# Low parts of the experts' weights made by VectorE alone, behind the first sixteen tiles

## The chip, the core and the metric

The kernel runs on one core of a Trainium2 chip. The time is the device time of one execution in microseconds (us), taken from the start of the program to its end. The core has a matrix engine (TensorE, PE in the profile), three elementwise engines (VectorE or DVE, ScalarE or ACT, GpSimd or POOL), an engine that issues most of the transfers (SyncE, SP) and 16 DMA engines. Each engine takes its instructions in a fixed order and stops at the first one whose inputs, or whose output buffer, are not ready.

## What is computed

An attention layer is followed by a mixture of experts. Of the reference, this is what matters:

```python
scores = scale * np.matmul(q, k.transpose(0, 1, 3, 2))       # q, k, v: 8 x 8 x 576 x 64
scores = np.where(causal, -1000000000.0, scores + np.minimum(bias, 0.0))
attn = softmax(scores);  attn_out = np.matmul(attn, v)
x = attn_out.transpose(0, 2, 1, 3).reshape(4608, 512)

logits = x @ w_gate + modality_bias[modality_id]             # 8 experts
e_idx = np.argmax(logits, axis=1)
gate_w = probs[np.arange(N), e_idx]
for e in range(8):
    mask = e_idx == e
    h = np.maximum(x[mask] @ w1[e], 0.0)                     # w1[e]: 512 x 1024
    out[mask] = gate_w[mask, None] * (h @ w2[e])             # w2[e]: 1024 x 512
```

Everything is float32. The matmuls run on rounded operands, so each operand is kept as two tiles: a high part (the value rounded to the matmul's type) and a low part (the value minus its high part). A product of two such operands is three matmuls: high by high, high by low and low by high.

## The kernel before

The attention fills the first 425 us. Meanwhile each token's row is written into a list in DRAM that belongs to its expert. The change touches only the second stage, the experts.

**Blocks.** The lists are worked off in blocks of 256 rows of one expert: 18 blocks (`N2` = 6, whose places are known early, and `N3` = 12), and then 2 quarter blocks of 64 rows (`NS`; a loop behind them for more has no iteration in this run). `Moe.run` goes through them. For each block `pre` reads the expert and the place from a table (`regs`), fetches the rows (`gather`, tile `xg`, and `oi`, the rows' places in the output, by VectorE at L856), and starts the fetch of the next block's weights.

**The weights.** The weights of one expert are eight chunks of 128x1024 (four of `w1`, four of `w2`), fetched anew for each block. `fetch` (L797, L799) issues one transfer of 512 KB into a raw tile, `wraw` (2 buffers) or `wrbw` (4 buffers). `parts` makes the two parts in one of thirteen tiles (`wca` 4, `wcb` 5, `wcc` 4, used in turn): ScalarE rounds the raw tile into the high part (L817), and VectorE or GpSimd subtracts the high part from the raw tile into the low part (L818). A raw tile is free for the next transfer when both have read it. Chunks are counted through from 1 (`n`); the first sixteen are those of the first two blocks and have a table of their own (`WDVE`); behind them the chunks with odd `j` go to VectorE and those with even `j` to GpSimd.

**A block.** `block` makes four tiles `hp` in PSUM (two buffers), each of 24 matmuls (L905). ScalarE takes the positive part as the high part of `hT` (L907), VectorE makes the low part (L908); a buffer of `hp` is free for the next but one tile when L908 has read it. `mid` transposes the next block's rows (PE L868) and splits them (ACT L870, DVE L871). `second` adds 48 matmuls (L884) into two tiles `y`; VectorE scales them (L890) and GpSimd issues the scatter of each to the output rows (L891). The fetch of the next but one block's rows overwrites the `xg` which L890 reads, so SyncE issues it (L843) behind L890, and the L856 that reads the new rows stands ahead of the second L908 on VectorE. A quarter block works with 64 rows (`quarter`, `sums`): hp in two tiles, L936, L947, the transposes L950, L952 and L953 for `hT`, then `y`.

**The routing in the third and fourth block.** `R.rest` (L711 on) computes the tables of the later blocks on VectorE, some 70 small instructions between the L908 of the third block and those of the fourth.

**What sets the order.** The order of each engine's instructions is set when the program is built, by the scheduler of the tile layer, from the order of the calls, from priorities (`high_priority`), from explicit marks (`issue_after`) and from its own estimates. A call that is put on another engine can therefore move other instructions.

Of the kernel before, what the change touches and what calls it, by code (L numbers as in the profile page):

```python
# [7 lines left out]
F32 = mybir.dt.float32  # L8
# [4 lines left out]
ALU = mybir.AluOpType  # L13
# [446 lines left out]
WDVE = (2, 4, 5, 6, 7, 9, 10, 12, 14, 16)  # L460
# [304 lines left out]
class Moe:  # L765
# [38 lines left out]
    def parts(self, raw, d, n, j):  # L804
        nc = self.nc
        m = n % (self.NA + self.NB + self.NC)
        if m < self.NA:
            w = self.wa.tile([P, 2, 1024], F32R, name="wca", bufs=self.NA)
        elif m < self.NA + self.NB:
            w = self.wb.tile([P, 2, 1024], F32R, name="wcb", bufs=self.NB)  # L810
        else:
            w = self.wc.tile([P, 2, 1024], F32R, name="wcc", bufs=self.NC)
        n += 1
        with ExitStack() as after:
            for i in self.tr[1:] if 4 < n <= 8 else ():
                after.enter_context(self.tc.issue_after(i.ins))
            nc.scalar.copy(w[:, 0], raw)  # L817
            (nc.vector if (j % 2 if n > 16 else n in WDVE) else nc.gpsimd).tensor_tensor(w[:, 1], raw, w[:, 0].bitcast(F32), ALU.subtract)  # L818
        return w, d

    def regs(self, tb, b):
# [101 lines left out]
    def sums(self, o, W, parts, scale=1.0):  # L923

        nc = self.nc
        n = len(parts)
        for i, (x, k, c0) in enumerate(parts):
            def low():
                nc.tensor.matmul(o[:64], x[:, :64], W[k][:, 1, c0:c0 + 512], start=False, stop=False)
            if i:  # L930
                low()
            self.last[0] = nc.tensor.matmul(o, x, W[k][:, 0, c0:c0 + 512], start=i == 0, stop=i == n - 1)
            if not i:
                low()
        lo = self.wc.tile([64, 512], F32, name="ql", bufs=2)
        self.last[3] = nc.scalar.activation(lo, o[64:], AF.Copy, scale=scale)  # L936
        return lo
# [165 lines left out]
```

## Time and profile before

| | us |
|---|---|
| three timed runs | 893.9, 898.71, 899.9; median 898.71 |
| the profiled execution | 901.84, of which its span 900.1 |
| busy in the span: PE / DVE / ACT / POOL | 833.4 / 633.0 / 527.3 / 574.1 |
| mean granted TensorE clock | 0.97 |

In the profile a row of the timeline gives start, duration, engine, line, operation, output<-inputs, shapes and count, and in brackets the idle time of the engine ahead of it with the instruction that ended it. A row of the windows gives, for a stretch from the span's start, its length and the busy time of PE, PE's weight load, DVE, ACT and POOL, then the granted clock, the DMA engines' mean busy share and the GB/s. A row of a source gives the count of such instructions and their shortest, median and longest duration in ns. A duration includes time in which the instruction stands and cannot move data.

### The profile page before, as it was taken

How to read it: one execution, taken by the hardware profiler on the slowest of the kernel's cores; microseconds unless marked ns; L12 is line 12 of the kernel's file. 1: busy time of each engine (PE TensorE's matmuls, PEld its weight loads, DVE VectorE, ACT ScalarE, POOL GpSimd, SP SyncE). 2: the span in 40 equal slices, each digit the busy share in tenths (PEclk: the TensorE clock that was granted, in tenths of full speed). 3: DMA queues.
4: the chain of work that ended last, by engine and by line, in shares of the span. 5: the costliest groups of instructions: out<-in, count | busy, mean ns of one | idle time of the engine just before them, and what ended most of it. 6: DMA issues, size and time to landing. Idle time of an engine off the chain costs nothing. (4 is left out here: it accounts for less than half of the span.)

```text
span 900.1 us, 16902 instructions
## 1 busy us (share of the span) xinstructions
PE 833.4 (93%) x5648; PEld 726.4 (81%) x5648; DVE 633.0 (70%) x1543; ACT 527.3 (59%) x1221; POOL 574.1 (64%) x471
## 2 busy tenths in 40 slices
PE   2889999997999899898989799999999999999984
PEld 2778888876887688686889698999999999999962
DVE  7668788877878688967748866666665666656681
ACT  5757888775877577677545244455554544444541
POOL 7767777778768787772556256565555655545860
PEclk9989999998999899989999999999999999999987
DMA  4563444534445444534878376666666666665840
GB/s 166 162 170 120 161 140 141 186 120 163 140 167 161 142 140 141 191 107 165 312 265 309 133 271 230 238 234 237 237 236 237 237 237 237 237 235 220 294 160 3
DMA packets 68888, 172.85 MB, mean 192 GB/s; under 512 B 13247, under 2 KB 13247, under 8 KB 68672
## 3 DMA queue, kind: packets, MB, share of 16 engines
q1 hardware_dynamic: 62944, 151.70, 48.8%
q0 software_dynamic: 5856, 20.06, 5.7%
q8 instruction: 45, 0.74, 0.3%
q14 instruction: 43, 0.35, 0.1%
HBM read 144.75 MB, written 26.80 MB: 191 GB/s over the span
## 5 line engine op out<-in xcount | busy, mean ns | idle before, releaser
L311 ACT ACTIVATE pe<-pe,mx 128x512 f32<-128x512 f32 (+3 forms) x256 | 143.5, 563 | 29.7 <-DVE mx L291 28.1
L291 DVE CUSTOM_DVE_ANT_0 pe<-sp,mk 128x512 f32<-128x512 f32 (+3 forms) x256 | 120.8, 485 | 28.1 <-PE sp L289 26.4
L324 ACT COPY PT<-pt 128x512 f32<-128x512 f32 (+3 forms) x256 | 104.4, 420 | 53.1 <-PE pt L321 50.1
L907 ACT ACTIVATE hT<-hp 128x512 fp32r<-128x512 f32 x72 | 42.8, 594 | 151.7 <-PE hp L905 147.9
L891 POOL DMA_INDIRECT out<-ys,oi x36 | 40.8, 1133 | 131.8 <-DVE ys L890 49.8
L321 PE MATMUL pt<-ident,pe 128*128 128x128 f32 x640 | 120.3, 287 | 1.5 <-ACT PT L324 1.5
L288 PE MATMUL sp<-KA,QH 128*128 128x256 f32 (+2 forms) x256 | 105.7, 416 | 15.2 <-POOL KA L168 10.4
L361 PE MATMUL o<-PT,V 128*64 128x320 f32 (+4 forms) x896 | 109.7, 373 | 3.5 <-DVE PT L340 3.4
L361 PEld LDWEIGHTS o<-PT,V 128*64 128x64 f32 x896 | 81.7, 140 | 36.4 <-DVE PT L340 15.8
L248 POOL TENSOR_TENSOR KA<-rawk,KA 64x576 fp32r<-64x576 f32 x62 | 88.0, 1434 | 24.9 <-DMA lists<-x,di 19.1
L905 PE MATMUL hp<-xT,wcb 128*128 128x256 f32 x648 | 90.0, 283 | 0.9 <-DVE hT L908 0.9
L321 PEld LDWEIGHTS pt<-ident,pe 128*128 128x128 f32 x640 | 78.9, 147 | 13.3 <-issue 5.6
L289 PE MATMUL sp<-KB,QL 76*128 76x256 f32 (+2 forms) x256 | 88.3, 347 | 0.8 <-POOL QL L250 0.7
L908 DVE SCALAR_TENSOR_TENSOR hT<-hp,hT 128x512 fp32r<-128x512 f32 x72 | 49.3, 684 | 53.0 <-ACT hT L907 52.9
L905 PEld LDWEIGHTS hp<-xT,wcb 128*128 128x128 f32 x648 | 83.5, 189 | 1.7 <-DVE hT L908 1.1
L905 PE MATMUL hp<-xT,wcc 128*128 128x256 f32 x528 | 76.5, 286 | 5.5 <-DVE hT L908 3.1
L884 PE MATMUL y<-wcb,hT 128*128 128x512 f32 x336 | 81.0, 398 | 0.0
L233 POOL TENSOR_SCALAR QH<-rawq 128x576 fp32r<-128x576 f32 x62 | 41.2, 682 | 60.5 <-issue 42.5
L905 PE MATMUL hp<-xT,wca 128*128 128x256 f32 x552 | 78.4, 285 | 0.4 <-ACT xT L870 0.3
L905 PEld LDWEIGHTS hp<-xT,wcc 128*128 128x128 f32 x528 | 69.6, 193 | 6.6 <-DVE hT L908 3.3
L884 PEld LDWEIGHTS y<-wcb,hT 128*128 128x128 f32 x336 | 62.9, 189 | 14.6
L905 PEld LDWEIGHTS hp<-xT,wca 128*128 128x128 f32 x552 | 72.2, 191 | 1.3 <-ACT xT L870 0.5
(271 smaller groups left out, 1952.4 us busy)
## 6 DMA issues: line engine op xcount, KB each, us to landing
wrbw<-in_w SPq DMA_DIRECT2D x104, 512.0 KB
wraw<-in_w SPq DMA_DIRECT2D x56, 512.0 KB
rawq<-in_qkv SPq DMA_DIRECT2D x32, 576.0 KB
rawk<-in_qkv SPq DMA_DIRECT2D x32, 576.0 KB
xg<-lists SPq DMA_DIRECT2D x18, 576.0 KB
V<-in_qkv SPq DMA_DIRECT2D x32, 320.0 KB
lists<-z SPq DMA_DIRECT2D x8, 576.0 KB
ekd<-ek SPq DMA_DIRECT2D x2, 720.0 KB
```

The costliest lines, as they stand in the source:

```text
L248: self.last = nc.gpsimd.tensor_tensor(KA[up, a], rk[up, a], KAf[up, a], ALU.subtract).ins
L288: self.pe.append(nc.tensor.matmul(sp[:, :nn], QH[:, q0:q0 + P], KA[:, ab, :nn], start=True, stop=False).ins)
L289: self.pe.append(nc.tensor.matmul(sp[:, :nn], QL[:EXT, q0:q0 + P], KB[:EXT, ab, :nn], start=False, stop=True).ins)
L291: ins = nc.vector.tensor_tensor_reduce(out=t[:, :n], in0=sp[:, :n], in1=self.mk[:, 512 - n:512], scale=-0.125, scalar=3.0e38, op0=ALU.add, ...
L311: self.act = nc.scalar.activation(t[:, :n], t[:, :n], AF.Exp, bias=m, scale=-1.0, accum_out=st["sums"][:, o:o + 1]).ins
L321: self.pe.append(nc.tensor.transpose(out=pt[:, P * j:P * j + P], in_=pe[:, P * j:P * j + P], identity=self.ident).ins)
L324: cp(w[:, :, v:v + P], pt[:, :P * (c + 1)].rearrange("p (j q) -> p j q", q=P))
L361: m = nc.tensor.matmul(o[r, f - q0:q1 - q0], V[:, ab, j, :], PT[ab][:, PTS * j + f if j < 4 else PTW - 64:PTS * j + q1 if j < 4 else PTW], ...
L884: self.last[0] = nc.tensor.matmul(y[u], hT[:, a, f, P * u:P * u + P], W[4 + f // 2][:, c, 512 * (f % 2):512 * (f % 2) + 512], start=f == 0 ...
L905: nc.tensor.matmul(hp[:, u], W[k][:, a, f:f + P], xT[:, c, k], start=k == 0 and i == 0, stop=k == 3 and i == 2)
L907: nc.scalar.activation(hs, hp, AF.Relu)
L908: nc.vector.scalar_tensor_tensor(hT[:, 1, 2 * m:2 * m + 2], hp, 0.0, hs.bitcast(F32), ALU.max, ALU.subtract)
```

## The change

Behind the first sixteen chunks L818 is VectorE's for each chunk; before, it was VectorE's for odd `j` and GpSimd's for even `j`. The first sixteen stay as they are. 160 chunks are made in this run, so 144 lie behind the first sixteen, and 72 of these L818 go from GpSimd to VectorE.

```diff
             nc.scalar.copy(w[:, 0], raw)
-            (nc.vector if (j % 2 if n > 16 else n in WDVE) else nc.gpsimd).tensor_tensor(w[:, 1], raw, w[:, 0].bitcast(F32), ALU.subtract)
+            (nc.vector if n > 16 or n in WDVE else nc.gpsimd).tensor_tensor(w[:, 1], raw, w[:, 0].bitcast(F32), ALU.subtract)
```

GpSimd's queue keeps the scatters (L891) alone from there on. SyncE's order is the same, ScalarE's moves in one place around the second block's end, TensorE's in the first quarter block by a few matmuls. VectorE's order moves throughout. In the fences below a row is an instruction with its line, output and inputs, in the order in which the engine takes them.

VectorE in the third block, between its third and its fourth L908 (the `r...` and `hn` tiles are the routing's). Before:

```order
L677 TENSOR_TENSOR rpast<-numf,rcn 128x38
L684 CAST rgi<-rbase 128x19
L744 TENSOR_SCALAR hn<-rcn 128x7
L678 TENSOR_SCALAR rpast<-rpast 128x38
L746 TENSOR_SCALAR hn_6483<-rcn 128x7
L818 TENSOR_TENSOR wcc<-wrbw,wcc 128x1024
L747 TENSOR_TENSOR hn<-hn,hn_6483 128x7
L746 TENSOR_SCALAR hn_6483<-rcn 128x7
L747 TENSOR_TENSOR hn<-hn,hn_6483 128x7
L746 TENSOR_SCALAR hn_6483<-rcn 128x7
L747 TENSOR_TENSOR hn<-hn,hn_6483 128x7
L908 SCALAR_TENSOR_TENSOR hT<-hp,hT 128x512
```

The same place now, from the first L818 behind the third L908 to the fourth L908:

```order
L818 TENSOR_TENSOR wcc<-wrbw,wcc 128x1024
L677 TENSOR_TENSOR rpast<-numf,rcn 128x38
L684 CAST rgi<-rbase 128x19
L744 TENSOR_SCALAR hn<-rcn 128x7
L678 TENSOR_SCALAR rpast<-rpast 128x38
L746 TENSOR_SCALAR hn_6483<-rcn 128x7
L818 TENSOR_TENSOR wca<-wrbw,wca 128x1024
L747 TENSOR_TENSOR hn<-hn,hn_6483 128x7
L818 TENSOR_TENSOR wca<-wraw,wca 128x1024
L746 TENSOR_SCALAR hn_6483<-rcn 128x7
L908 SCALAR_TENSOR_TENSOR hT<-hp,hT 128x512
```

Three L818 stand ahead of the fourth L908 where one stood, and three routing instructions that stood ahead of it stand behind it.

VectorE in a later full block, from its second L908 to its two L890. Before:

```order
L908 SCALAR_TENSOR_TENSOR hT<-hp,hT 128x512
L818 TENSOR_TENSOR wcc<-wrbw,wcc 128x1024
L908 SCALAR_TENSOR_TENSOR hT<-hp,hT 128x512
L818 TENSOR_TENSOR wcc<-wrbw,wcc 128x1024
L908 SCALAR_TENSOR_TENSOR hT<-hp,hT 128x512
L871 TENSOR_TENSOR xT<-tp,xT 128x512 x2
L818 TENSOR_TENSOR wca<-wraw,wca 128x1024
L818 TENSOR_TENSOR wca<-wrbw,wca 128x1024
L890 TENSOR_SCALAR ys<-y,xg_9048 128x512 x2
```

The same block now, from behind its second L908:

```order
L818 TENSOR_TENSOR wcb<-wrbw,wcb 128x1024
L818 TENSOR_TENSOR wcc<-wrbw,wcc 128x1024
L908 SCALAR_TENSOR_TENSOR hT<-hp,hT 128x512
L818 TENSOR_TENSOR wcc<-wraw,wcc 128x1024
L818 TENSOR_TENSOR wcc<-wrbw,wcc 128x1024
L908 SCALAR_TENSOR_TENSOR hT<-hp,hT 128x512
L871 TENSOR_TENSOR xT<-tp,xT 128x512
L818 TENSOR_TENSOR wcc<-wrbw,wcc 128x1024
L818 TENSOR_TENSOR wca<-wraw,wca 128x1024
L871 TENSOR_TENSOR xT<-tp,xT 128x512
L818 TENSOR_TENSOR wca<-wrbw,wca 128x1024 x2
L890 TENSOR_SCALAR ys<-y,xg_9048 128x512 x2
```

Two L818 stand where one stood, ahead of the third L908, of the fourth, of the second L871 and of the L890; the first two L908 of a block have none new ahead of them.

VectorE in the first quarter block. Before:

```order
L890 TENSOR_SCALAR ys<-y,xg_10032 128x512 x2
L947 TENSOR_TENSOR hs<-hp,ql 64x512
L818 TENSOR_TENSOR wca<-wrbw,wca 128x1024
L953 SCALAR_TENSOR_TENSOR hT<-tp,hT 128x4x64
L947 TENSOR_TENSOR hs<-hp,ql 64x512
```

Now:

```order
L890 TENSOR_SCALAR ys<-y,xg_10032 128x512 x2
L818 TENSOR_TENSOR wca<-wraw,wca 128x1024
L947 TENSOR_TENSOR hs<-hp,ql 64x512
L818 TENSOR_TENSOR wca<-wrbw,wca 128x1024 x2
L953 SCALAR_TENSOR_TENSOR hT<-tp,hT 128x4x64
L947 TENSOR_TENSOR hs<-hp,ql 64x512
```

One more L818 stands ahead of each of the first L947 and the first L953.

## The prediction, made before the changed kernel was run

> **What bounds the kernel now.** I read the page first (PE busy 93% of the span), then the windows, to see where TensorE is not busy from the third block on, for which the first moved chunk is made; nothing ahead of that moves.
>
> ```profile
> 500.00:520.00 20.00, 15.40 (x98) 14.06 (x97) 15.22 (x39) 2.24 (x3) 3.80 (x3) 0.91 0.39 146
> 520.00:560.00 40.00, 39.09 (x237) 34.53 (x236) 27.22 (x23) 21.16 (x26) 25.79 (x11) 1.00 0.68 255
> 560.00:840.00 280.00, 280.00 (x1811) 254.09 (x1811) 176.50 (x157) 137.22 (x170) 160.60 (x73) 1.00 0.64 236
> 840.00:865.00 25.00, 25.00 (x157) 22.18 (x156) 17.94 (x15) 13.02 (x16) 19.41 (x8) 1.00 0.75 260
> 865.00:880.00 15.00, 12.73 (x50) 8.22 (x49) 10.68 (x11) 6.42 (x10) 7.59 (x4) 0.77 0.20 74
> ```
>
> From 560 to 865 us TensorE has no gap, at a clock of 1.00: no faster VectorE or GpSimd can shorten that stretch, though most of the moved instructions lie in it. What is to be won lies at 500 to 560 and behind 865. TensorE's waits from 460 us on are these three groups, all on VectorE:
>
> ```profile
> PE hp L905 <- DVE hT L908: 4.0, 2, 3.1
> PE y L932 <- DVE hT L953: 2.8, 2, 2.3
> PE y L884 <- DVE hT L908: 1.5, 1, 1.5
> ```
>
> 8.3 us in all. A block's starts on TensorE tell what the first two groups cost with what follows them:
>
> ```profile
> 480.24 0.51 PE L905 MATMUL hp<-xT,wca 128*128 128x256 f32 x3
> ...
> 503.21 2.61 PE L884 MATMUL y<-wcc,hT 128*128 128x512 f32 x10 [1.54 <-DVE hT L908]
> 505.66 0.87 PE L905 MATMUL hp<-xT,wcc 128*128 128x256 f32 x6
> ...
> 514.62 1.16 PE L905 MATMUL hp<-xT,wcc 128*128 128x256 f32 x6 [3.05 <-DVE hT L908]
> 515.57 1.49 PE L905 MATMUL hp<-xT,wca 128*128 128x256 f32 x6
> ...
> 534.05 1.24 PE L905 MATMUL hp<-xT,wcb 128*128 128x256 f32 x9
> ...
> 543.72 1.34 PE L905 MATMUL hp<-xT,wcb 128*128 128x256 f32 x9 [0.91 <-DVE hT L908]
> ...
> 558.76 1.24 PE L905 MATMUL hp<-xT,wca 128*128 128x256 f32 x9
> ...
> 841.06 1.24 PE L905 MATMUL hp<-xT,wcb 128*128 128x256 f32 x9
> ```
>
> The sixth block starts at 558.76 and the eighteenth at 841.06: 282.30 / 12 = 23.53 us each, undisturbed. The third (480.24 to 505.66) takes 25.42, the fourth 28.39, the fifth 24.71: 1.89, 4.86 and 1.18 too long. The fourth loses more than its wait, since the six matmuls behind it take 1.16 to 1.49 us instead of 0.87.
>
> Why is VectorE late there? Its rows and GpSimd's:
>
> ```profile
> 484.00:514.00 30.00, 26.02 (x170) 23.28 (x169) 29.62 (x72) 12.04 (x15) 11.15 (x6) 1.00 0.58 217
> ```
>
> ```profile
> 480.41 2.17 DVE L818 TENSOR_TENSOR wcc<-wrbw,wcc 128x1024 fp32r<-128x1024 f32 x1
> ...
> 489.82 2.37 DVE L734 TENSOR_TENSOR rs<-rs,numf 128x19 f32<-128x19 f32 x1
> ...
> 492.79 2.40 DVE L738 SCALAR_TENSOR_TENSOR rbase<-rex,rs 128x19 f32<-128x19 f32 x1
> ...
> 496.06 0.16 DVE L746 TENSOR_SCALAR hn<-rcn 128x7 f32<-128x7 f32 x1
> 496.13 1.21 DVE L818 TENSOR_TENSOR wcc<-wrbw,wcc 128x1024 fp32r<-128x1024 f32 x1
> ...
> 497.45 2.27 DVE L746 TENSOR_SCALAR hn<-rcn 128x7 f32<-128x7 f32 x1
> ...
> 499.96 2.40 DVE L746 TENSOR_SCALAR hn<-rcn 128x7 f32<-128x7 f32 x1
> ...
> 502.47 0.68 DVE L908 SCALAR_TENSOR_TENSOR hT<-hp,hT 128x512 fp32r<-128x512 f32 x1
> ...
> 513.88 0.68 DVE L908 SCALAR_TENSOR_TENSOR hT<-hp,hT 128x512 fp32r<-128x512 f32 x1
> ```
>
> ```profile
> 489.65 2.51 POOL L818 TENSOR_TENSOR wcc<-wraw,wcc 128x1024 fp32r<-128x1024 f32 x1 [2.39 <-ACT wcc L817]
> 492.69 2.46 POOL L818 TENSOR_TENSOR wca<-wrbw,wca 128x1024 fp32r<-128x1024 f32 x1 [0.53 <-ACT wca L817]
> 497.29 2.41 POOL L818 TENSOR_TENSOR wca<-wrbw,wca 128x1024 fp32r<-128x1024 f32 x1 [2.14 <-ACT wca L817]
> 499.95 2.38 POOL L818 TENSOR_TENSOR wcb<-wraw,wcb 128x1024 fp32r<-128x1024 f32 x1 [0.25 <-ACT wcb L817]
> ```
>
> VectorE is busy 29.62 of 30 us. The same L746 on 7 elements takes 0.16 us at 496.06 and 2.27 and 2.40 later; each long one begins within 0.2 us of a GpSimd L818 and ends with it. L818 on VectorE takes 1.21 us where GpSimd is idle.
>
> **The change part by part.**
>
> *L818 itself.* 72 move. Their price on VectorE has two bounds, from the source's row:
>
> ```profile
> L818 DVE TENSOR_TENSOR wcb<-wrbw,wcb x21: 1206/2246/3411, 428.1 to 858.2; 128x1024 fp32r<-128x1024 f32 x21
> ```
>
> 1.21 us is the shortest, 2.25 the median with GpSimd beside it. With GpSimd left to the scatters I take 1.21 for all. A block's eight then cost 9.7 us and, with four L908 (0.68 each, 2.7), two L871 and two L890 (taken like L908, 2.7) some 15 of 23.5 us: no bound. At 2.25 it would be 23.4, the whole block; no row has such a duration without a GpSimd L818 beside it, so that end is not taken.
>
> *The third and fourth block.* Five instructions lose their standstill: 2.37 + 2.40 + 2.27 + 2.40 - 4 x 0.16 = 8.8, and 2.17 - 1.21 = 1.0 for the L818 at 480.41. The four GpSimd L818 quoted come to VectorE: 4 x 1.21 = 4.8. Three to six short routing instructions go behind an L908 (about 1 us). VectorE's queue up to the fourth block's first L908 shortens by 9.8 - 4.8 + 1 = 6.0: from 513.88 to about 508, or to 509 or 510 if a late high part (ScalarE's L817, itself waiting for a transfer) holds one of the L818 now ahead. The third block's last L908 goes from 502.47 to about 497 (8.8 + 1.0 less three added L818 and a wait or two); TensorE stood for it until 503.21, having come at 501.67, so that wait goes, and the block loses its whole excess: **1.9 us**. The fourth block then starts at 503.8 and needs its first L908 half-way through its hp matmuls, 5.9 us after its start (before: 505.66 to 511.57, where the 3.05 us wait begins): at 509.7. What is late next is this same L908 (0 to 0.9 us), and the second one, which stands behind L856 and so behind the rows' transfer. I leave 0.7 us of the block's 4.86: **4.2 us**. That the slow matmuls go with the 3.05 us wait is part of it.
>
> *The fifth block.* Its wait has the same shape:
>
> ```profile
> 533.11 3.02 DVE L818 TENSOR_TENSOR wca<-wraw,wca 128x1024 fp32r<-128x1024 f32 x1 [0.33 <-ACT wca L817]
> ...
> 536.05 1.40 DVE L890 TENSOR_SCALAR ys<-y,xg 128x512 f32<-128x512 f32 x2
> ...
> 542.90 0.16 DVE L856 TENSOR_TENSOR oi<-xg,no 128x2 int32<-128x2 f32 x1 [4.46 <-DMA xg<-lists]
> ```
>
> L890 started 2.0 us behind the end of the fourth block's matmuls (534.05), because the L818 ahead of it took 3.02 us. L890 releases the transfer that L856 waits for, and the second L908 stands behind L856. With L818 at 1.2 us it comes over 1 us earlier and the 0.91 us wait goes: **1.0 us** of 1.18.
>
> *From 560 to 865.* Cover: TensorE's queue. The added L818 stand ahead of the third and fourth L908 and the L890, never ahead of the first two L908, on which the hp buffers hang. If the cover went, VectorE would have to be late by more than the slack below (rival three). Charged nothing.
>
> *The quarter blocks.*
>
> ```profile
> 867.97 2.69 DVE L818 TENSOR_TENSOR wca<-wrbw,wca 128x1024 fp32r<-128x1024 f32 x1 [0.28 <-ACT wca L817]
> 870.58 0.41 DVE L953 SCALAR_TENSOR_TENSOR hT<-tp,hT 128x256 fp32r<-128x256 f32 x1
> ```
>
> One L818 of 2.69 us becomes two of 1.2 ahead of L953: it comes 0.3 us earlier, and TensorE still waits about 2 us of its 2.3, with the slow matmuls behind (clock 0.77). **0.3 us**.
>
> *GpSimd* loses 72 instructions on no path; its scatters can come earlier or stand behind a VectorE L818. Nothing of TensorE's waits names them: nothing.
>
> Sum: 1.9 + 4.2 + 1.0 + 0.3 = 7.4 us. The profiled execution, 901.84, becomes 894.4; it lay 3.1 above the median of the timed runs, 898.71, from which the forecast is 891.3.
>
> The Trainium skill has a rule that speaks against the change ("Perfetto Trace Analysis", Optimizing Scalar/DVE Operations): if VectorE is saturated, offloading some work to other engines, even GpSimd, may make sense. By that alone the four L818 brought back into the saturated 484 to 514 us would make the fourth block 4.8 us later, the time 903. The same section adds that the two engines share a port, so that moving work between them might not help; "SBUF — State Buffer" (SBUF: two separate sides) has that port as an exclusive lock, held for the whole instruction. The four long rows above are such standstills, so the trace sides with the lock.
>
> **The rivals.** *One: the relief is eaten* (0.16). The L818 now in the routing's queue wait for late high parts, which wait for transfers, and the fourth block keeps its wait. For it: VectorE takes them in order. Against: they stand there about as late as on GpSimd before. Only the third and fifth block gain: 2 to 3 us, time 896.
>
> *Two: the tail goes too* (0.13). If L953 comes before TensorE needs it, its 2.3 us go, and with them the slow clock behind: at 0.77 over the window's 15 us at most 0.23 x 15 = 3.4 us, of which I take 2.2. 7.4 + 4.5 = 12, time 887. Against: two L818 stand ahead of it and the second's high part is late itself.
>
> *Three: slower, by VectorE's order in every block* (0.07). Where the last L818 ahead of L890 waits for its high part, the next rows' transfer, L856 and the second L908 follow late. The slack:
>
> ```profile
> 671.18 1.05 ACT L817 CAST wcc<-wraw 128x1024 fp32r<-128x1024 f32 x1 [0.29 <-DMA wraw<-in_w]
> ...
> 675.84 1.45 DVE L890 TENSOR_SCALAR ys<-y,xg 128x512 f32<-128x512 f32 x2 [0.45 <-PE y L884]
> ```
>
> The last high part is there at 672.2, its L818 done at 673.5, L890 begins at 675.84: 2.3 us of slack. From there on each microsecond of lateness costs one per block: 1 us over the twelve blocks 12, time 911.
>
> *Four: the standstills are not GpSimd's* (0.06): 4.8 us more on VectorE in the fourth block, time 903.
>
> **How the numbers follow.** The forecast has 0.58: a gain of 4 to 10 us. The timed runs lie 893.9 to 899.9, so the median moves some 3 us by itself; about 1% (9 us) is what tells a change from none. Range: low end rival two with 2 us of that, 885; high end rival one with 3, 899; rivals three and four lie outside. Faster by over 1% (below 889.7): rival two and a quarter of the forecast, 0.13 + 0.14 = 0.27. Slower: rival three, 0.07. Within 1%: 0.66.
>
> **What would show it.** After the change: L818 on VectorE at 1.2 us, median too; no L734, L738 or L746 over 0.3 us; the fourth block's wait under 1 us; the sixth to eighteenth block still 23.5 us each; L953 near its old place. It is wrong if L818 stays near 2.2 us, if a wait on L908 or on weights appears between 560 and 865, or if the third to fifth block keep more than 2 us over 23.53 each.

## The result, and the profile after

| | before | after |
|---|---|---|
| runs, median (us) | 6 runs, 899.62 (893.9 to 903.19) | 6 runs, 889.65 (883.67 to 890.95) |
| ratio of the times | | 0.9875, 95% interval 0.983 to 0.9919 |
| profiled execution, its span | 901.84, 900.1 | 889.8, 888.1 |
| busy: PE / DVE / ACT / POOL | 833.4 / 633.0 / 527.3 / 574.1 | 826.3 / 625.9 / 529.1 / 370.3 |
| granted TensorE clock | 0.97 | 0.979 |

VectorE took over 72 subtractions and is busy for 7.1 us less. 2.5 us of that lie ahead of the first moved one (354.3 and 351.8 us); from there on it is busy for 278.7 us before and 274.1 after. The subtractions alone would have raised that: its own 72 fell from 163.2 to 87.9 us, by 75.3, and the 72 new ones cost 88.0. The short instructions make up for it: L746, L856, L738 and L734 together take 12.8 us less, by their durations. (Busy time counts instructions once where their records overlap, so such sums do not add up to it.) The windows of the changed kernel, with the columns of the ones before (length; PE, weight load, DVE, ACT, POOL; clock, DMA share, GB/s):

```profile
484.00:514.00 30.00, 30.00 (x201) 27.36 (x200) 24.81 (x64) 14.98 (x20) 1.97 (x2) 1.00 0.78 293
500.00:520.00 20.00, 20.00 (x137) 18.39 (x136) 15.02 (x32) 11.17 (x14) 1.97 (x2) 1.00 0.88 322
520.00:560.00 40.00, 40.00 (x276) 37.01 (x275) 24.44 (x29) 17.57 (x24) 3.94 (x4) 1.00 0.65 237
560.00:840.00 280.00, 280.00 (x1811) 253.93 (x1810) 178.70 (x206) 136.95 (x170) 23.62 (x24) 1.00 0.65 237
840.00:860.00 20.00, 18.09 (x80) 12.98 (x78) 16.78 (x19) 12.47 (x16) 2.47 (x2) 0.96 0.50 166
```

TensorE has no gap from 484 to 840 us. Of its waits behind the third block's start one group is left:

```profile
PE y L932 <- DVE hT L953: 2.4, 2, 1.9
```

The starts of the third to the sixth block on TensorE in the changed kernel, by its timeline:

```profile
475.81 0.51 PE L905 MATMUL hp<-xT,wca 128*128 128x256 f32 x3
...
499.41 0.87 PE L905 MATMUL hp<-xT,wcc 128*128 128x256 f32 x6
...
522.89 1.24 PE L905 MATMUL hp<-xT,wcb 128*128 128x256 f32 x9
...
546.43 1.24 PE L905 MATMUL hp<-xT,wca 128*128 128x256 f32 x9
```

The three blocks take 23.60, 23.48 and 23.54 us, where they took 25.42, 28.39 and 24.71: 7.90 us less. The next two fences give VectorE's L818 and L746 by source, then its timeline around the fourth block's start:

```profile
L818 DVE TENSOR_TENSOR wcb<-wrbw,wcb x39: 1214/1224/1227, 423.5 to 845.0; 128x1024 fp32r<-128x1024 f32 x39
L746 DVE TENSOR_SCALAR hn<-rcn x3: 164/168/169, 488.4 to 492.9; 128x7 f32<-128x7 f32 x3
```

```profile
490.92 0.69 DVE L908 SCALAR_TENSOR_TENSOR hT<-hp,hT 128x512 fp32r<-128x512 f32 x1
...
503.13 0.69 DVE L908 SCALAR_TENSOR_TENSOR hT<-hp,hT 128x512 fp32r<-128x512 f32 x1
...
506.23 0.16 DVE L856 TENSOR_TENSOR oi<-xg,no 128x2 int32<-128x2 f32 x1 [1.47 <-DMA xg<-lists]
506.30 0.68 DVE L908 SCALAR_TENSOR_TENSOR hT<-hp,hT 128x512 fp32r<-128x512 f32 x1
```

L818 takes 1.22 us in its median, not 2.25, and no L746 stands still. The fourth block's first L908 ends at 503.8; with that block's start at 499.41 and 5.9 us from start to need (the prediction's count), TensorE wants it at 505.3.

At the tail little changed. TensorE's wait for L953 is 1.91 us instead of 2.27, and the slow matmuls behind it (0.43 us from start to start, against 0.23 at full clock) are still there:

```profile
855.96 0.49 PE L932 MATMUL hp<-wcb,xT 128*128 128x512 f32 x1
858.37 0.79 PE L932 MATMUL y<-wcb,hT 128*128 128x512 f32 x1 [1.91 <-DVE hT L953]
...
864.14 0.63 PE L929 MATMUL y<-wcb,hT 128*64 128x512 f32 x1
864.57 0.63 PE L932 MATMUL y<-wcb,hT 128*128 128x512 f32 x1
...
865.53 0.40 PE L929 MATMUL y<-wcb,hT 128*64 128x512 f32 x1
```

The two profiled spans differ by 12.0 us, of which the change can have made only a part: the third block already started at 475.81 instead of 480.24 us, 4.43 earlier. This lead is there at the first block's start, at 422.03 instead of 426.62, before the first moved L818 (464.10 us in the changed kernel). Four of the moved L818 (chunks 17, 19, 21 and 23) do lie ahead of the third block's start, within the second block, but that block takes 28.10 us here and 27.94 before, so they gained nothing there. From the third block's start to the end of the span it is 419.86 us before and 412.29 after. These 7.57 us are called the gain of the **stretch** below; the experiments are read by it as well as by their times.

### The profile page after: what moved, and what is told of

It is laid out like the page before. It is cut to its first block, busy times and chain, and to the rows that moved or that the text cites. A ratio compares the mean times of both kernels' runs of the same rounds, so it can differ in the third digit from the quotient of the medians.

```text
span 888.1 us, 16783 instructions
## 1 busy us (share of the span) xinstructions
PE 826.3 (93%) x5648; PEld 720.3 (81%) x5648; DVE 625.9 (70%) x1615; ACT 529.1 (60%) x1221; POOL 370.3 (42%) x399
## 5 line engine op out<-in xcount | busy, mean ns | idle before, releaser
L891 POOL DMA_INDIRECT out<-ys,oi x36 | 37.6, 1045 | 365.9 <-DVE ys L890 261.9
L311 ACT ACTIVATE pe<-pe,mx 128x512 f32<-128x512 f32 (+3 forms) x256 | 143.9, 565 | 27.8 <-DVE mx L291 25.6
L361 PE MATMUL o<-PT,V 128*64 128x320 f32 (+4 forms) x896 | 107.7, 368 | 2.7 <-DVE PT L340 2.6
L361 PEld LDWEIGHTS o<-PT,V 128*64 128x64 f32 x896 | 79.9, 138 | 35.5 <-DVE PT L340 14.5
L908 DVE SCALAR_TENSOR_TENSOR hT<-hp,hT 128x512 fp32r<-128x512 f32 x72 | 49.5, 688 | 54.1 <-ACT hT L907 54.1
L288 PEld LDWEIGHTS sp<-KA,QH 128*128 128x128 f32 x256 | 49.7, 195 | 18.0 <-POOL KA L168 10.3
```

The lines of the kernel that those rows point to most:

```text
L288: self.pe.append(nc.tensor.matmul(sp[:, :nn], QH[:, q0:q0 + P], KA[:, ab, :nn], start=True, stop=False).ins)
L311: self.act = nc.scalar.activation(t[:, :n], t[:, :n], AF.Exp, bias=m, scale=-1.0, accum_out=st["sums"][:, o:o + 1]).ins
L361: m = nc.tensor.matmul(o[r, f - q0:q1 - q0], V[:, ab, j, :], PT[ab][:, PTS * j + f if j < 4 else PTW - 64:PTS * j + q1 if j < 4 else PTW], ...
L908: nc.vector.scalar_tensor_tensor(hT[:, 1, 2 * m:2 * m + 2], hp, 0.0, hs.bitcast(F32), ALU.max, ALU.subtract)
```

## The experiments

The theory: GpSimd's L818 makes VectorE's instructions stand still, and where VectorE is full (third to fifth block) TensorE waits for it; elsewhere VectorE has room and the change does nothing. The rivals: the gain comes from shorter L818 in all the blocks; it comes from the new order of VectorE's queue, not from GpSimd's silence; more of it could be had in the second block or at the tail. The table has each kernel's profiled execution, worked out from the starts on TensorE (us):

| kernel | third block's start | third | fourth | fifth | first quarter | stretch | median time | ratio to before |
|---|---|---|---|---|---|---|---|---|
| before | 480.24 | 25.42 | 28.39 | 24.71 | 13.95 | 419.86 | 899.62 | |
| before, again | 478.78 | 23.73 | 29.72 | 24.85 | 13.04 | 418.72 | 898.02 | 1.0017 |
| changed | 475.81 | 23.60 | 23.48 | 23.54 | 14.01 | 412.29 | 889.65 | 0.9875 |
| changed, again | 475.00 | 23.86 | 24.50 | 23.54 | 12.60 | 412.20 | 888.87 | 0.9902 |
| changed, third time | 478.40 | 23.60 | 23.48 | 23.54 | 14.04 | 412.30 | 892.42 | 0.9932 |
| only chunks 17 to 41 | 476.12 | 23.62 | 24.51 | 23.54 | 13.18 | 412.28 | 890.57 | 0.9931 |
| only chunks behind 41 | 476.62 | 24.93 | 29.14 | 25.12 | 12.55 | 419.08 | 897.57 | 0.9995 |
| GpSimd writes a constant | 478.71 | 23.61 | 23.47 | 23.54 | 10.17 | 408.49 | 884.62 | 0.9842 |
| GpSimd copies | 479.62 | 23.60 | 24.48 | 23.54 | 10.18 | 409.48 | 889.94 | 0.9896 |
| three early chunks too | 476.01 | 23.60 | 24.23 | 23.54 | 12.58 | 411.59 | 888.69 | 0.9887 |
| both quarters earlier | 476.49 | 23.60 | 23.46 | 23.54 | (new order) | 413.31 | 894.09 | 0.9953 |
| first quarter earlier | 472.74 | 23.69 | 24.23 | 23.54 | (new order) | 410.86 | 888.64 | 0.9916 |

**The change for the third to fifth block's chunks alone.**

```diff
-            (nc.vector if n > 16 or n in WDVE else nc.gpsimd).tensor_tensor(...)
+            (nc.vector if (n <= 41 or j % 2 if n > 16 else n in WDVE) else nc.gpsimd).tensor_tensor(...)
```

> Only the chunks 17 to 41 (third, fourth and fifth block, one of the sixth) have all low parts on VectorE; behind them VectorE and GpSimd take turns as before. Theory (the gain is the standstills in the third to fifth block): those blocks take 23.5 to 24 us each on TensorE, the stretch from the third block's start to the end of the span is 412.6 us (changed kernel 412.3, before 419.9), the time about 0.3 us above the changed kernel's. Rival (each moved low part helps a little): about a fifth of the gain, the stretch at 418 us.

Ratio 0.9931 (0.9897 to 0.9965), stretch 412.28, the changed kernel's being 412.29. That they agree to a hundredth is luck: the fourth block is 1.0 us longer here and the quarter blocks 1.0 us shorter, and both vary as much in the changed kernel itself. Behind chunk 41 GpSimd's turns are back and VectorE's L818 are long again, yet the sixth to eighteenth block keep their 23.5 us. Its groups by form, from 470 to 900 us:

```profile
L818 DVE TENSOR_TENSOR wcb<-wrbw,wcb 128x1024 fp32r<-128x1024 f32 x20 | 39.7, 1990 | 15.9 <-ACT wcb L817 15.8
...
L818 POOL TENSOR_TENSOR wcb<-wrbw,wcb 128x1024 fp32r<-128x1024 f32 x15 | 40.6, 2710 | 9.3 <-ACT wcb L817 7.8 <-PE tp L868 1.4
```

The cover that the prediction named for 560 to 865 us is real: long L818 there cost nothing.

**Its complement: only the chunks behind the forty-first.**

```diff
-            (nc.vector if n > 16 or n in WDVE else nc.gpsimd).tensor_tensor(...)
+            (nc.vector if (n > 41 or j % 2 if n > 16 else n in WDVE) else nc.gpsimd).tensor_tensor(...)
```

> The complement: chunks 17 to 41 take turns as before, all behind them on VectorE. Theory: the third to fifth block keep 25.4, 28.4 and 24.7 us, the stretch from the third block's start to the end is 419.5 us, within 0.5 us of before. Rival (each moved low part helps): four fifths of the gain, the stretch at 414 us.

Ratio 0.9995 (0.9978 to 1.0011), stretch 419.08, within 0.8 us of before. 59 of the 72 moved instructions are worth nothing measurable. TensorE's waits from 470 to 560 us, and VectorE's and GpSimd's rows that make them:

```profile
PE hp L905 <- DVE hT L908: 5.3, 3, 3.0
PE hp L905 <- DVE xT L871: 0.5, 1, 0.5
```

```profile
488.24 1.98 DVE L735 TENSOR_SCALAR rs<-rs 128x19 f32<-128x19 f32 x1
...
491.04 2.07 DVE L677 TENSOR_TENSOR rpast<-numf,rcn 128x38 f32<-128x38 f32 x1
...
495.96 1.97 DVE L637 TENSOR_TENSOR_SCAN hinc<-hn,zero 128x7 f32<-128x7 f32 x1
...
498.45 2.07 DVE L639 TENSOR_TENSOR hexc<-hinc,hn 128x7 f32<-128x7 f32 x1
```

```profile
487.80 2.39 POOL L818 TENSOR_TENSOR wcc<-wraw,wcc 128x1024 fp32r<-128x1024 f32 x1 [2.60 <-ACT wcc L817]
490.65 2.40 POOL L818 TENSOR_TENSOR wca<-wrbw,wca 128x1024 fp32r<-128x1024 f32 x1 [0.47 <-ACT wca L817]
495.48 2.42 POOL L818 TENSOR_TENSOR wca<-wrbw,wca 128x1024 fp32r<-128x1024 f32 x1 [2.43 <-ACT wca L817]
498.09 2.40 POOL L818 TENSOR_TENSOR wcb<-wraw,wcb 128x1024 fp32r<-128x1024 f32 x1 [0.19 <-ACT wcb L817]
```

Here not L734, L738 and L746 stand still but L735, L677, L637 and L639: each ends with the GpSimd L818 beside it, and together they lose 7.4 us (their sum less 0.17 each). Which instruction is caught differs from one execution to the next. The cost is one standstill for each GpSimd L818.

**GpSimd keeps its turns but writes a constant.** VectorE's queue is that of the kernel before.

```diff
-            (nc.vector if n > 16 or n in WDVE else nc.gpsimd).tensor_tensor(...)
+            nc.gpsimd.memset(w[:, 1].bitcast(F32), 1.0e-4) if n > 16 and j % 2 == 0 else (nc.vector if n > 16 or n in WDVE else nc.gpsimd).tensor_tensor(...)
```

> VectorE's queue is word for word that of the kernel before; where GpSimd made a low part behind the first sixteen it writes a constant of the same size instead, reading nothing. Left out: those low parts. Theory (the standstill is GpSimd's reading low part, and VectorE's load of low parts is not what counts): L734, L738 and L746 at 0.2 us, L818 on VectorE at 1.2 us, the third to fifth block at 23.5 to 24 us each, the stretch from the third block's start to the end near 412.5 us, as in the changed kernel. Rival (any long GpSimd instruction stops VectorE's): rows above 0.5 us beside GpSimd's constant, the fourth block's wait stays above 1 us, the stretch above 415 us.

Ratio 0.9842 (0.9813 to 0.987). The three blocks take 23.61, 23.47 and 23.54 us, with VectorE's order unchanged and its number of L818 as before. So the new order is not the cause. The four L818 that the change puts into the routing's queue can be free: with them (changed) and without them (here) the fourth block takes 23.48 and 23.47. They are not always: of the seven executions in the table that have them there, three show 23.46 to 23.48 and four 24.22 to 24.51 (one of these is shown below). The standstills did not go altogether. VectorE's rows beside two memsets (on GpSimd from 489.79 to 490.74 and from 490.68 to 491.71):

```profile
489.99 0.78 DVE L684 CAST rgi<-rbase 128x19 int32<-128x19 f32 x1
490.07 0.71 DVE L744 TENSOR_SCALAR hn<-rcn 128x7 f32<-128x7 f32 x1
490.14 0.66 DVE L678 TENSOR_SCALAR rpast<-rpast 128x38 f32<-128x38 f32 x1
490.23 0.58 DVE L746 TENSOR_SCALAR hn<-rcn 128x7 f32<-128x7 f32 x1
490.50 1.23 DVE L818 TENSOR_TENSOR wcc<-wrbw,wcc 128x1024 fp32r<-128x1024 f32 x1
```

Four short instructions with one input wait together until about 490.8; the L818 with two inputs is not touched. At the tail this kernel goes further than the change: TensorE waits 1.10 us for L953, no slow matmuls follow, and the first quarter block takes 10.17 us instead of 14.01.

```profile
860.46 0.49 PE L932 MATMUL y<-wcb,hT 128*128 128x512 f32 x1 [1.10 <-DVE hT L953]
860.79 0.62 PE L929 MATMUL y<-wcb,hT 128*64 128x512 f32 x2
```

**GpSimd copies instead of subtracting.**

```diff
-            (nc.vector if n > 16 or n in WDVE else nc.gpsimd).tensor_tensor(...)
+            nc.gpsimd.tensor_copy(w[:, 1], raw) if n > 16 and j % 2 == 0 else (nc.vector if n > 16 or n in WDVE else nc.gpsimd).tensor_tensor(...)
```

> As in the memset run, GpSimd keeps its turns behind the first sixteen and VectorE's queue is that of the kernel before, but GpSimd copies the raw weights into the place of the low parts (one operand read, one written) instead of subtracting two operands; those low parts are left out of the computation, raw weights stand in their place. If VectorE stands still beside any GpSimd instruction that reads SBUF, L746 or its neighbours take 1 to 2 us again for as long as the copy takes, and the third to fifth block take about 25, 28 and 25 us. If only GpSimd's two-operand subtraction does it, no short VectorE instruction takes over 0.5 us there, the blocks take 23.6, 23.5 and 23.5 us, and the time is near the changed kernel's.

Ratio 0.9896 (0.9862 to 0.9931), and both expectations were half right. VectorE stands still again, here in two-input instructions:

```profile
492.83 1.00 DVE L747 TENSOR_TENSOR hn<-hn,hn 128x7 f32<-128x7 f32 x1
...
495.83 0.96 DVE L639 TENSOR_TENSOR hexc<-hinc,hn 128x7 f32<-128x7 f32 x1
...
498.45 1.19 DVE L649 TENSOR_TENSOR hoh<-hoh,ha 128x196 f32<-128x196 f32 x1
```

but for 1.0 us, the length of a copy on GpSimd (1.04 to 1.24 us here), not 2.4. With a fourth (L656, 0.4 us too long) they lose 2.9 us instead of 7.4 to 8.8, which the queue nearly has room for: 23.60, 24.48 and 23.54 us, with one wait of 0.74. What made the kernel before slow is the number of GpSimd's instructions times their length, in a place where VectorE is full.

**Three chunks of the second block to VectorE as well.**

```diff
-WDVE = (2, 4, 5, 6, 7, 9, 10, 12, 14, 16)
+WDVE = (2, 4, 5, 6, 7, 9, 10, 11, 12, 13, 14, 15, 16)
```

> The changed kernel, and in addition the low parts 11, 13 and 15 (second block) on VectorE; they stood on GpSimd behind nine scatters of the routing. Theory: the second block, 28.1 us from start to start in the changed kernel against 23.5 undisturbed, loses its two waits of 2.0 and 0.7 us and most of the slow matmuls behind: 24 to 25 us, the time 3 to 4 us below the changed kernel. Rival (the high parts and transfers are late anyway): under 1 us.

The rival was right: ratio 0.9887 (0.9863 to 0.9912), like the changed kernel. The second block takes 27.42 us; in the executions with the old table it took 26.3 to 28.7. The waits of the changed kernel from 445 to 478 us, then those of this one:

```profile
PE hp L905 <- POOL wcc L818: 2.0, 1, 2.0
PE hp L905 <- DVE wcc L818: 0.7, 1, 0.7
```

```profile
PE hp L905 <- ACT wcc L817: 2.3, 1, 2.3
PE hp L905 <- DVE wcc L818: 0.9, 1, 0.9
```

The wait only moves on by one chunk. The low part that TensorE waited for (of chunk 11, by GpSimd) is early now, but the high part of the next chunk is late: ScalarE makes it from 451.00 us on (449.61 in the changed kernel), behind 6.55 us of waiting for a transfer. So the limit there is not who subtracts.

**The changed kernel a second time.**

> The changed kernel once more, unaltered, for two numbers that one profiled execution leaves open. First, the gain: if only the third to fifth block gain, as the traces have it (419.86 to 412.29 us from the third block's start to the span's end), the medians of paired runs differ by 7 to 8 us, ratio near 0.992; the rival is that the 10 us by which the first comparison's medians differ are the change's, ratio near 0.989. Second, the third block's start, which lay at 480.24 and 475.81 us in the two profiles with the same instructions ahead: if that is chance of the execution, it lies anywhere between 475 and 481 again; the stretch behind it is 411 to 413 us.

Ratio 0.9902 (0.9869 to 0.9936); stretch 412.20; the third block starts at 475.00. The fourth block takes 24.50 us here. Its timeline on VectorE and on TensorE:

```profile
489.07 1.21 DVE L818 TENSOR_TENSOR wca<-wrbw,wca 128x1024 fp32r<-128x1024 f32 x1
491.27 1.23 DVE L818 TENSOR_TENSOR wca<-wraw,wca 128x1024 fp32r<-128x1024 f32 x1 [0.91 <-ACT wca L817]
...
504.29 0.68 DVE L908 SCALAR_TENSOR_TENSOR hT<-hp,hT 128x512 fp32r<-128x512 f32 x1
```

```profile
505.03 0.98 PE L905 MATMUL hp<-xT,wcc 128*128 128x256 f32 x6 [0.33 <-DVE hT L908]
508.30 0.97 PE L905 MATMUL hp<-xT,wcc 128*128 128x256 f32 x6 [0.15 <-DVE hT L908]
```

An L818 in the routing's queue waits 0.91 us for a late high part, and L908 comes 0.33 us late. This is rival one's mechanism, at a small size: 0.48 us of waits instead of 3.05, and 1.0 us in the block. The four longer fourth blocks of the table all have it: that L818 waits 0.75 to 0.93 us, and L908 begins 29.0 to 29.3 us behind the third block's start; in the other three it waits 0.55 us at most, and L908 begins at 27.3 to 28.0.

**The quarter blocks earlier in the order**, first both, then the first alone.

```diff
-            with (self.tc.high_priority(offset=PRI) if early and k == 0 else ExitStack()):
+            with (self.tc.high_priority(offset=PRI) if early and k == 0 or lst[k][2] == 1 and len(lst) > 1 else ExitStack()):
```

> The changed kernel, with the first quarter block's first layer and transposes put earlier in the written order (the block gets the scheduler's high priority), so that its two hidden-state copies L953 stand on VectorE right behind the eighteenth block's L890, and the L818 of the last weights behind or ahead of that. Theory (the 1.9 us wait on L953 and the slow matmuls behind it are a matter of VectorE's order and still to be had): no wait of TensorE on L953 over 0.5 us at the first quarter block, the way from the first quarter's first layer to the second quarter's about 10 us instead of 14, the stretch from the third block's start to the end of the span 408 to 409 us instead of 412.29, the time 3 to 4 us below the changed kernel's. Rival (the last weights' high and low parts, which are late themselves, set the tail): the wait moves to hp or y on a late wca or wcc, the stretch stays above 411, the time within 1.5 us of the changed kernel's.

Theory wrong, by the stretch (413.31) and the time (ratio 0.9953, 0.9928 to 0.9978). TensorE waits 0.71 us for xT and 1.29 us around the first quarter, with no slow matmuls behind; at the second quarter it stands for L947, and matmuls at half speed follow:

```profile
870.34 0.43 PE L950 MATMUL tp<-ident,hs 64*128 64x64 f32 x4 [2.25 <-DVE hs L947]
...
872.15 1.05 PE L929 MATMUL y<-wca,hT 128*64 128x512 f32 x2
```

Presumably the two quarters have nothing left to overlap with; no run shows that. The median lies 5 us above the changed kernel's of the same comparison, the stretch 1.1; the rest of that is not explained.

```diff
-            with (self.tc.high_priority(offset=PRI) if early and k == 0 else ExitStack()):
+            with (self.tc.high_priority(offset=PRI) if early and k == 0 or len(lst) > 1 and lst[k][2] == 1 and lst[k - 1][2] == 2 else ExitStack()):
```

> The changed kernel with only the first of the two quarter blocks put earlier in the written order; the second stays where it is in the changed kernel. In the run with both put earlier TensorE waited about 2 us in all around the first quarter, with no slow matmuls behind it, and 2.25 us on L947 of the second. Theory (that second wait came from the second quarter's place in the order, and the first quarter's gain was real): waits of about 2 us around the first quarter, none over 0.6 us and no slow matmuls behind it, stretch from the third block's start to the span's end 409 to 411 us, time 1 to 3 us below the changed kernel's. Rival (the first quarter's gain is given back at the second, whatever its place): a wait of over 2 us or slow matmuls show up at the second quarter, the stretch is 412 us or more, the time that of the changed kernel or above.

With the first alone no wait behind it is over 0.5 us and the matmuls stay fast. The stretch is 410.86, 1.4 us below the changed kernel's three (412.20 to 412.30), in the expected range. The times, 888.64 us (883.21 to 893.52, 8 runs) against 892.42 (884.49 to 892.97, 9 runs) of the changed kernel beside it, overlap: that it is the faster of the two is what the one profile says; the times do not show it.

**Before again, and the changed kernel a third time**, beside it.

> The kernel before once more, unaltered: a second profiled execution of it. Theory (what the change gains lies behind the third block's start, and what lies ahead of it varies with the execution): third to fifth block again near 25.4, 28.4 and 24.7 us, the stretch from the third block's start to the span's end 419 to 420 us, the third block's start anywhere between 475 and 481 us, near the middle of what the eight kernels with the same code ahead of it showed (475.0 to 480.2). Rival (the change also shortens what lies ahead): the third block starts near 480 again, later than in any changed kernel.

> The changed kernel again, beside the two above on the same chip: 888 to 891 us, stretch 411 to 413 us; its first quarter block takes 12.5 to 14 us, according to how long TensorE's matmuls stay slow behind the 1.9 us wait on L953.

Before: three blocks of 23.73, 29.72 and 24.85 us, 78.3 in all as in the first profile (78.5), stretch 418.72, start of the third block 478.78. Changed: stretch 412.30, ratio 0.9932 (0.9903 to 0.9961). The third block's start did come later than in every changed kernel, as the rival had it: 476.62 to 480.24 us in the five profiled executions with GpSimd's turns, 472.74 to 478.40 in the seven where VectorE makes the third block's low parts, with one overlap (476.62). But the split is there at the first block's start already (424.5 to 427.3 against 420.8 to 424.0), and up to there VectorE, ScalarE and GpSimd have the same instructions in all twelve. The granted clock differs with it: ahead of the first block's start it stood at one half for 30.7 us in the profile of before and for 17.1 us in that of the changed kernel; which of the two makes the other is open. The medians do not repeat the split: less the stretch, they are 476.1 to 480.5 us in the five and 476.7 to 480.8 in the seven. The changed kernel's three medians lie 10.0, 9.3 and 4.8 us below those of before in the same comparison, its stretches 6.4 to 7.7 us below the two of before. All 21 runs of it have a median of 890.07 and all 58 of before beside them 898.09, 8.0 us apart. So about 7 us are the stretch's, and the 10 us of the first comparison were partly scatter. Whether the last microsecond is the change's stays open.

## Why the prediction was right

The forecast was 891.3 us, from a gain of 7.4; measured were 889.65 in the first comparison and 890.07 over all runs, and a gain of 7.57 us in the two profiled stretches.

| term | forecast | measured, profiles before and changed |
|---|---|---|
| third block | 1.9 | 25.42 - 23.60 = 1.82 |
| fourth block | 4.2 | 28.39 - 23.48 = 4.91 (3.89 in the second execution) |
| fifth block | 1.0 | 24.71 - 23.54 = 1.17 |
| 560 to 865 us | 0 | 0: from the sixth block's start to the first quarter 305.6 us in both |
| quarter blocks | 0.3 | 13.95 + 21.84 - 14.01 - 22.10 = -0.3 |

That the sum came within 0.2 us is in part luck: the fourth block gave 0.7 more than its term and the quarter blocks 0.6 less.

*What lies ahead of the third block.* "Nothing ahead of that moves" is a misreading: four of the moved L818 are made during the second block. The sum is not touched, since the second block takes 27.55 and 27.94 us before and 26.97 to 28.71 in the changed kernel's three.

*L818 at 1.21 us.* Right: 1.22 in the median. The upper bound, 2.25 us, was rightly not taken; the kernel with the first blocks' chunks alone shows that such durations come back with GpSimd's turns.

*The queue of the third and fourth block.* It was to shorten by 6.0 us, with L908 beginning 27.8 us behind the third block's start or up to 2 us later. It began at 503.13 - 475.81 = 27.3, and at 29.3 in the second execution, where one L818 waited for its high part. The 0.7 us left in the block stand between what the executions show: no excess in two of the changed kernel's three, 1.0 in the third, and 0.45 on average over the seven with these L818 in the queue. That wait costs less than the 3.05 us did, since the matmuls behind it stay fast (0.97 and 0.98 us for six, against 1.16 to 1.49).

*The third block's last L908* was put at about 497, 16.8 us behind that block's start; it came 15.1 behind it, and 17.5 in the second execution. It was no longer awaited in either.

*The fifth block.* Right in mechanism and size: L818 at 1.2 us, no wait.

*The quarter blocks.* The wait fell by 0.36 us, as forecast, but the slow matmuls lasted longer: from the end of the wait to the second quarter's first matmul 7.6 us instead of 7.2. The term has the wrong sign, because its working left out where the slow clock falls, which matters more than the term. In both profiles it lasts 6.83 us, but before 0.8 us of that passed while TensorE still waited; in the changed kernel's second execution it lasts 3.41 us, and the first quarter takes 12.60 us instead of 14.01.

*The rivals.* One appeared at a small size, as said. Two did not happen in the changed kernel; its prize of 4.5 us was about right, since the kernel whose GpSimd writes a constant has a first quarter 3.8 us shorter. Three: no wait between 560 and 840 us. Four is refuted by the constant: with VectorE's queue as it was and GpSimd's operation alone exchanged, the long rows go.

*The two rules of the Trainium skill.* The trace and the runs side with the lock in "SBUF — State Buffer" against offloading in "Perfetto Trace Analysis": taking work back to a VectorE that was 29.62 of 30 us busy made its queue shorter.

*The chances.* Faster by over 1% had 0.27. The first comparison came out there (0.9875), the two later ones at 0.9902 and 0.9932, just inside 1%: the effect lies close to the bound, where the forecast had put it.

## What to carry to other kernels

Before giving an elementwise engine's work to GpSimd, look in the timeline for VectorE instructions that are much longer than their shortest form and end together with a GpSimd instruction: that busy time is waiting, and taking the work back can lower VectorE's load. Then ask where VectorE is the one that TensorE waits for. Of 72 instructions moved here only those of three blocks out of twenty paid, and they are found by comparing each block's length with an undisturbed one.

## What the runs showed of the hardware

*What stands still beside what.* Worked out from all VectorE instructions from 400 us on that overlap a GpSimd L818 by over 0.1 us. Beside GpSimd's subtraction (two inputs) 63 of 65 L818 on VectorE took 1.6 to 3.5 us instead of 1.2, and short instructions from SBUF to SBUF up to 2.4 instead of 0.16, while the 33 L908, which read PSUM for one of their inputs, stayed at 0.67 to 0.69. Beside its copy (one input) only 7 of 45 L818 took longer, up to 2.79 us; there it is mostly GpSimd that stands, since 28 of the 72 copies took 1.4 to 2.1 us instead of 1.04, each of them beside an L818 of VectorE. Beside its memset (no input) all 27 L818 kept 1.22 to 1.23, and only short one-input instructions stood, for 0.4 to 0.65 us. The prediction had taken any GpSimd instruction for a lock on VectorE; that a write alone holds up VectorE's short one-input instructions and not its two-input ones was not in it. The Trainium skill has just this in "SBUF — State Buffer" (Who interferes with whom): two SBUF inputs contend only with a GpSimd instruction that reads SBUF, and an instruction with at most one SBUF input not at all unless it runs in a mode that uses both ports. The 27 and 65 L818 and the 33 L908 agree with it.

*Slow matmuls behind a wait.* In the third to fifth block and at the tail, TensorE's waits of 1.10, 1.29 and 1.54 us left its matmuls fast; behind 1.91, 2.25, 2.27 and 3.05 us they ran at about half speed. In the second block that order breaks: the wait of 2.30 us in the kernel with three early chunks was followed by matmuls at full speed, that of 1.99 us in the changed kernel by matmuls at half speed. The record of the granted clock tells them apart. Its stretches of full and of half clock last 3.41 us or a multiple of that (but for the last, which the span's end cuts), so each execution has a fixed grid of such windows. Over the twelve traces, all 53 windows at full clock in which TensorE was busy for less than 1.6 us were followed by a window at half clock, none of the 2807 in which it was busy for more than 2.0 us, and 17 of the 37 between. The two waits by these windows, first the changed kernel, then the one with three early chunks:

```profile
448.73:452.14 3.41, 0.79 (x4) 0.59 (x5) 1.45 (x2) 2.53 (x3) 2.37 (x2) 1.00 0.01 5
452.14:455.55 3.41, 3.41 (x17) 3.41 (x18) 3.11 (x5) 0.72 (x2) 3.25 (x2) 0.50 0.35 80
```

```profile
448.19:451.60 3.41, 1.61 (x12) 1.33 (x10) 0.00 (x0) 0.59 (x1) 0.00 (x0) 1.00 0.45 181
451.60:455.01 3.41, 2.03 (x15) 1.84 (x16) 2.93 (x3) 2.35 (x3) 0.00 (x0) 1.00 0.00 0
```

The shorter wait lies in one window with the one behind it, the longer is split over two. The Trainium skill ("TensorE: Matmul & The Clock Gate", What's actually happening) has the clock halve after an idle window of about 3.4 us, in a window that runs freely. The window's length agrees; but the window need not be idle here, since less than half of it busy was enough. At the tail the step from 1.9 to 1.1 us of wait came with 3.8 us less for the first quarter block, so there a wait may be worth shortening even if it can't be removed.
